# Float32 blocks first in each group of attention's value products

## The chip, the cores and the metric

The kernel runs on one core of one Trainium2 chip. The metric is device time in microseconds, the median of several runs. A profile of one execution stands beside them: for every instruction its engine, its start and its length. The engines are PE (matrix products, with its weight loads shown as PEld), DVE (vector work), ACT (activation functions, here mainly the exponential), POOL (general work) and SP (which starts DMAs).

## The reference

One input `x` of 2048 tokens by 640 features is normalised, goes through multi-head attention and through an MLP with a second normalisation, and all three are added up.

```
xn = _layernorm(x, axis=-1)
return x + _A_ref(xn, A_wqkv, A_wo) + _B_ref(xn, B_w1, B_b1, B_w2, B_b2)

# _A_ref: 32 heads of 20 features
scores = jnp.einsum("bhqd,bhkd->bhqk", q, k) * (Dh ** -0.5)
p = _softmax(scores, axis=-1)
o = jnp.einsum("bhqk,bhkd->bhqd", p, v)
```

`_B_ref` is a layer norm, a dense layer to 1536 features, GELU, and a dense layer back to 640.

## The kernel before

The kernel computes at about float32 accuracy. Most operands are split into an upper and a lower 16-bit half, and a product is the sum of several 16-bit products.

A first part normalises, transposes and projects to q, k and v. V goes to the tile `vfull`, by key blocks of 128 tokens: `SPLIT` (L25) marks two blocks of every four as split. A split block holds V as two float16 halves, the other two hold it as float32. With each head's 20 columns goes a column of ones, so that the products also give the softmax's sum.

Then comes attention, with the MLP and the output projection filled in between. Heads go in pairs: `(g, hf)` is a pair of heads and a half of the queries, `cc` one of two chunks of 512 queries in it, and `kb` a key block. A **unit** is one key block for one pair and one chunk. `scores` (L594) makes two products into a PSUM tile `s` (`psS` has three buffers) and ACT's exponential of it into a float32 tile `p` (L602), from the pool `ptp`, which has `2 * GRP - 1`, seven, buffers. For a split block, `rest` (L609) lets DVE subtract from `p` its upper bf16 half; the remainder is `low`, float16, with four buffers.

The **value products** of four units, a group (`GRP`), are made at once by `pv` (L619). All add up in one PSUM bank `o`, in four strips of 32 partitions: strip `q` has head `a = q // 2` of the pair, and `q % 2` keeps apart two partial sums. A product uses 32 columns of weights from `vfull`, so products on four strips can run side by side. For each split block and head there are two upper products (the upper half of `p`, read as bf16, with both halves of V) and one lower product (`low` with the upper half of V). A float32 block has one float32 product for each head. That makes 8 upper, 4 lower and 4 float32 products for a group, 256 groups in all. `start` is set on the first product of each strip in an accumulation over 16 blocks; after the last, ACT copies `o` to `ev` (L652).

The order around it is written out by hand. After scores of the second block of a group come the subtraction for the first block and a portion of filler (`other`); after scores of the fourth come the subtraction for the second block and then `pv(prev)`, the products of the group before. Filler is bounded by a credit, which grows by `rate` once a group. Filler is MLP work on PE (L823, L855) with its GELU on DVE and ACT (L758 to L770), and later the projection (L932).

So when the fourth exponential of a group is issued, the group's other three `p` tiles are in use and the four of the group before too. It takes the one that comes free first, by the order of the products in `pv(prev)`; the next three exponentials take the others in the order in which they come free. This is the loop:

```
for g, hf, cc, kb0 in groups:
    units = []
    for kb in range(kb0, kb0 + GRP):
        units.append([g, hf, cc, kb, scores(g, hf, cc, kb)])
...
        else:
            for u in units[1:]:
                rest(u)
            if prev:
                pv(prev)
...
    prev = units
```

Of the kernel before, what the change touches and what calls it, by code (L numbers as in the profile page):

```python
# [42 lines left out]
def mha_mlp_kernel(tc, x, wqkv, wo, w1, b1, w2, b2, out):  # L43
# [4 lines left out]
    with (  # L48
# [21 lines left out]
        vfull = keep.tile([P, PAD + NKB * VROW], F32, name="vfull")  # L70
# [441 lines left out]
        with ExitStack() as scope:  # L512
# [92 lines left out]
            def upper(pt):  # L605

                return pt.bitcast(BF16).rearrange("p a (n t) -> p a n t", t=2)[:, :, :, 1]
# [11 lines left out]
            def pv(units):  # L619

                g, hf, cc, kb0 = units[0][:4]
                if kb0 == 0:
                    pv.o = psO.tile([P, 512], F32, tag="o", name="o")
                    pv.begun = set()
                last = units[-1][3] == NKB - 1

                def product(q, src, v0, t):  # L630
                    nc.tensor.matmul(pv.o[32 * q : 32 * q + 32, :], src[:, v0 - PAD * (1 - q % 2) :][:, :32], t,  # L631
                                     start=q not in pv.begun, stop=last, skip_group_check=True)
                    pv.begun.add(q)

                split = [(u[3], upper(u[4]), u[5]) for u in units if SPLIT[u[3]]]
                whole = [(u[3], u[4]) for u in units if not SPLIT[u[3]]]
                of16 = lambda kb, a: 2 * PAD + kb * 2 * VROW + (2 * g + a) * 2 * VW
                of32 = lambda kb, a: PAD + kb * VROW + (2 * g + a) * VW
                for kb, up, _ in split:
                    for a in range(2):  # L640
                        product(2 * a, vhalf, of16(kb, a), up[:, a])
                        product(2 * a + 1, vhalf, of16(kb, a) + VW, up[:, a])
                for a in range(2):
                    for n, (kb, _, low) in enumerate(split):
                        product(2 * a + n % 2, vhalf, of16(kb, a), low[:, a])
                for a in range(2):
                    for n, (kb, pt) in enumerate(whole):
                        product(2 * a + n % 2, vfull, of32(kb, a), pt[:, a])
                if last:
                    if cc == 0:  # L650
                        evs[g, hf] = m1.tile([P, 2, 512], F32, tag="ev", name="ev")
                    nc.scalar.activation(evs[g, hf][:, cc], pv.o, AF.Copy)  # L652
                    if cc == 1:
                        unload(g, hf, evs.pop((g, hf)))
# [5 lines left out]
            def unload(g, hf, ev):  # L660
                cols = slice(hf * 1024, (hf + 1) * 1024)
                for p in range(2):
                    dma(g, hf)(lpart[p, hf, 2 * g : 2 * g + 2, :].rearrange("a (c t) -> a c t", c=2),
                                      ev[PAD + DH + VW * p :: 64])
                    for a in range(2):
                        q0, r = 64 * a + PAD + VW * p, (2 * g + a) * DH
                        dma(g, hf)(opart[p, r : r + DH, cols].rearrange("d (c t) -> d c t", c=2),
                                          ev[q0 : q0 + DH])
                if g + 1 in ENDS:
                    fins.append(finish(g + 1 - UNITS[ENDS.index(g + 1)], g + 1, hf))  # L670
                    if len(fins) == 1:

                        (sides if hf == 1 and g + 1 >= TAIL else patient).append(finishing())
# [289 lines left out]
            with tc.manual_schedule():  # L963
# [18 lines left out]
# [4 lines that stand above are left out]
                        if kb % 2 == 0:  # L986
                            continue
                        tick()
                        if kb % GRP == 1:

                            rest(units[0])
                            credit += rate
                            other()
# [7 lines that stand above are left out]
                                credit += rate  # L1003
                                other()
                    prev = units
                    if cc == 0 and kb0 == 0 and (g, hf) != ORDER[-1]:
                        n = ORDER[ORDER.index((g, hf)) + 1]
                        sides.append(load_stack(*n, *([stacks[g, hf][1]] if n[0] == g else [])))
                n = 0
# [12 lines left out]

                more(2)
                pv(prev)
                while more(1):
                    pass
# [102 lines left out]
```

## Time and profile before

| | us |
|---|---|
| median of three runs | 1376.91 (1376.67 to 1377.99) |
| the profiled execution, as timed | 1378.13 |
| its span in the profile | 1376.4 |
| PE busy | 1347.3 |
| ACT busy | 1125.5 |
| DVE busy | 1061.0 |

How to read the rows in what follows. A row of a group of instructions has the line of the kernel, the engine, the operation, the tile written and the tiles read, the shapes and the count; then the busy time in us and the mean length of one in ns; then the idle time of the engine just before, with what ended it. A row of waits has who waited for whom, the sum in us, the number of times and the longest. A row of the timeline has start and length in us, and equal neighbours merged with their count. A row of a window has its length and each engine's busy time in the order PE, PEld, DVE, ACT, POOL, then the granted clock of PE, the share of the DMA engines and GB/s. Ends of matrix products are modelled and neighbours overlap, so a short wait of PE can be hidden inside busy time.

### The profile page before, as it was taken

Reading aid. Unit: us, or ns where it says so; the run is one execution under the profiler, and the core shown is the slowest. Engines: PE = TensorE matmul, PEld = TensorE weight load, DVE = VectorE, ACT = ScalarE, POOL = GpSimd, SP = SyncE. Lnnn points to the kernel's source line nnn. Section 1 sums busy time; section 2 is a strip of 40 time slices with the busy share of each in tenths; the row PEclk is TensorE's granted clock in tenths of the full one; section 3 lists DMA queues with packets and bytes.
Section 4 is the critical chain, followed back from the end, with each engine's and each line's share of the span. In section 5 each row is a group of like instructions: output and inputs, shape, how many; then the busy total and the mean of one; then the engine's idle time right before and its main releaser. Section 6 shows DMA issues by size and latency. Waiting matters only on the chain.

```text
span 1376.4 us, 29091 instructions
## 1 busy us (share of the span) xinstructions
PE 1347.3 (98%) x11711; PEld 599.3 (44%) x11711; DVE 1061.0 (77%) x1425; ACT 1125.5 (82%) x1282; POOL 32.6 (2%) x75
## 2 busy tenths in 40 slices
PE   8999998999999999999999999999999999999998
PEld 6555555443334333433343333343434434333375
DVE  6647753899778988788888778887978898898732
ACT  5644332999999999999999999999999999999700
POOL 2000000000000000000000000000000000000000
PEclk9999999999999999999999999999999999999999
DMA  9853413012113222213231123232123222244275
GB/s 266 226 187 115 99 58 114 3 33 62 52 38 100 81 76 68 70 47 82 67 99 40 47 66 89 64 83 62 41 57 113 73 76 77 65 135 119 89 235 177
DMA packets 92320, 125.68 MB, mean 91 GB/s; under 512 B 16905, under 2 KB 58569, under 8 KB 92178
## 3 DMA queue, kind: packets, MB, share of 16 engines
q1 hardware_dynamic: 89218, 117.14, 28.9%
q0 software_dynamic: 2304, 5.24, 2.2%
q8 instruction: 94, 1.54, 0.5%
q10 hardware_dynamic: 656, 1.36, 0.3%
q14 instruction: 48, 0.39, 0.1%
HBM read 80.84 MB, written 42.86 MB: 90 GB/s over the span
## 4 chain that ended last, share of the span: by engine, by line
PE 66%; DVE 8%; ACT 3%; DMA 2%; issue 2%; SPq 1%; DVEq 0%; ACTq 0%
PE o L631 26%; PE s L600 16%; PE py L855 11%; PE pu L823 9%; PE z L932 4%; DVE low L614 3%; ACT p L602 3%; DVE u L758 1%; DVE u L759 1%; DVE w L762 1%; DMA oscr<-oa 1%; DMA acc<-accscr 0%; DVE w L763 0%; DVE hT L770 0%; DVE u L768 0%
## 5 line engine op out<-in xcount | busy, mean ns | idle before, releaser
L602 ACT ACTIVATE p<-s 128x1024 f32<-128x1024 f32 x1024 | 973.9, 1043 | 46.2 <-PE s L600 38.9
L614 DVE TENSOR_TENSOR low<-p 128x1024 f16<-128x1024 f32 x512 | 610.6, 1218 | 162.4 <-ACT p L602 161.7
L631 PE MATMUL o<-p,vfull 128*32 128x512 bf16 (+1 forms) x4096 | 430.2, 493 | 0.0
L600 PE MATMUL s<-qs,ks 61*128 61x512 f16 x2048 | 317.3, 382 | 7.0 <-ACT p L602 5.5
L600 PEld LDWEIGHTS <-ks 61*128 61x128 f16 x2048 | 64.0, 94 | 294.4 <-issue 291.9
L823 PE MATMUL pu<-xm,w1t 128*128 128x256 f16 x1440 | 181.1, 275 | 3.8 <-DMA xm<-xscr 2.7
L855 PE MATMUL py<-w2t,hT 128*128 128x320 f16 x1152 | 178.6, 300 | 1.7 <-DVE u L758 1.1
L823 PEld LDWEIGHTS <-w1t 128*128 128x128 f16 x1440 | 131.5, 98 | 72.1 <-issue 57.8
L855 PEld LDWEIGHTS <-hT 128*128 128x128 f16 x1152 | 102.5, 98 | 89.3 <-issue 55.1
L286 PE MATMUL qkp<-xnt,wv 128*128 128x512 f16 x600 | 132.5, 379 | 0.2 <-DVE wv L383 0.2
L631 PEld LDWEIGHTS <-vfull 128*32 128x32 f16 x3072 | 60.4, 95 | 137.7 <-issue 106.3
L631 PE MATMUL o<-low,vfull 128*32 128x512 f16 x1024 | 103.5, 378 | 3.7 <-DVE low L614 3.7
L300 ACT ACTIVATE qkhl<-qkp,qks 128x1024 f16<-128x1024 f32 (+1 forms) x24 | 23.3, 971 | 82.9 <-PE qkp L286 65.4
L286 PEld LDWEIGHTS <-wv 128*128 128x128 f16 x600 | 58.1, 98 | 68.2 <-DVE wv L383 0.7
L631 PEld LDWEIGHTS o<-p,vfull 128*32 128x32 f32 x2048 | 62.1, 108 | 52.3
L932 PE MATMUL z<-w1t,ot 128*128 128x320 f16 x480 | 66.3, 299 | 1.4 <-DMA ot<-oscr 0.8
L349 PE MATMUL vp<-wv,xnt 128*128 128x320 f16 x480 | 66.6, 299 | 0.0
L932 PEld LDWEIGHTS <-ot 128*128 128x128 f16 x480 | 46.5, 98 | 21.9 <-issue 2.9
L349 PEld LDWEIGHTS <-xnt 128*128 128x128 f16 x480 | 46.5, 98 | 18.2
L893 DVE SCALAR_TENSOR_TENSOR acc<-z,sc,acc 128x320 f32<-128x320 f32 x32 | 17.5, 550 | 46.8 <-PE z L932 42.7
L301 DVE SCALAR_TENSOR_TENSOR qkhl<-qkp,qks,qkhl 128x1024 f16<-128x1024 f32 (+1 forms) x24 | 26.5, 1104 | 32.2 <-ACT qkhl L300 32.2
L652 ACT ACTIVATE ev<-o 128x512 f32<-128x512 f32 x64 | 39.5, 618 | 3.5 <-PE o L631 3.5
(168 smaller groups left out, 682.6 us busy)
## 6 DMA issues: line engine op xcount, KB each, us to landing
qkscr<-qkhl SPq DMA_DIRECT2D x40, 256.0 KB
opart<-ev SPq DMA_DIRECT2D x124, 80.0 KB
ks<-qkscr SPq DMA_DIRECT2D x120, 80.0 KB
qs<-qkscr SPq DMA_DIRECT2D x192, 40.0 KB
oa<-opart SPq DMA_DIRECT2D x32, 240.0 KB
xt<-in_A_x_dram SPq DMA_DIRECT2D x16, 320.0 KB
xscr<-xnt SPq DMA_DIRECT2D x4, 1280.0 KB
xm<-xscr SPq DMA_DIRECT2D x8, 640.0 KB
```

The lines of the kernel that those rows point to most:

```text
L286: nc.tensor.matmul(ps[:, i, :], wv[:, k, q, a, mm * P : (mm + 1) * P], xnts[c][:, k, b, :], start=(k + n == 0), stop=(k == KD - 1 and n == 2))
L300: nc.scalar.activation(hl[:, 0, i0:i1], ps[:, i0:i1], AF.Copy, scale=a)
L301: nc.vector.scalar_tensor_tensor(hl[:, 1, i0:i1], ps[:, i0:i1], a, hl[:, 0, i0:i1], ALU.mult, ALU.subtract)
L349: nc.tensor.matmul(ps[:, hf, :320], xnts[c][:, k, a, j * P : (j + 1) * P], wv[:, k, 2, b, hf * 320 : (hf + 1) * 320], start=(n == 0), stop ...
L600: nc.tensor.matmul(ps[:, a, :], ks[64 * a : 64 * a + 61, kb * P : (kb + 1) * P], qs[64 * a : 64 * a + 61, cc * 512 : (cc + 1) * 512], star ...
L602: nc.scalar.activation(pt, ps, AF.Exp, scale=QS)
L614: nc.vector.tensor_sub(low, pt, upper(pt))
L631: nc.tensor.matmul(pv.o[32 * q : 32 * q + 32, :], src[:, v0 - PAD * (1 - q % 2) :][:, :32], t, start=q not in pv.begun, stop=last, skip_gr ...
L652: nc.scalar.activation(evs[g, hf][:, cc], pv.o, AF.Copy)
L823: nc.tensor.matmul(ps[:, i], w1v[:, k, (f + i) // 4, a, fo_ : fo_ + P], xnt[:, k, b, :], start=(n == 0), stop=(n == 3 * KD - 1))
L855: nc.tensor.matmul(ps[:, :320], hTs[mc][:, f, a, j * P : (j + 1) * P], w2v[:, f, b, hf * 320 : (hf + 1) * 320], start=(n == 0), stop=(n == ...
L932: nc.tensor.matmul(ps[:, :320], ot[:, k, a, j * P : (j + 1) * P], wov[:, k, b, h * 320 : (h + 1) * 320], start=(n == 0), stop=(n == 3 * KD ...
```

## The change

In `pv`, the loop over the float32 blocks is moved from the end to the beginning. The order in a group was upper, lower, float32; it becomes float32, upper, lower. The products are the same, with the same operands.

```diff
                 of32 = lambda kb, a: PAD + kb * VROW + (2 * g + a) * VW
+                for a in range(2):
+                    for n, (kb, pt) in enumerate(whole):
+                        product(2 * a + n % 2, vfull, of32(kb, a), pt[:, a])
                 for kb, up, _ in split:
                     for a in range(2):
                         product(2 * a, vhalf, of16(kb, a), up[:, a])
                         product(2 * a + 1, vhalf, of16(kb, a) + VW, up[:, a])
                 for a in range(2):
                     for n, (kb, _, low) in enumerate(split):
                         product(2 * a + n % 2, vhalf, of16(kb, a), low[:, a])
-                for a in range(2):
-                    for n, (kb, pt) in enumerate(whole):
-                        product(2 * a + n % 2, vfull, of32(kb, a), pt[:, a])
```

## The prediction

> **What bounds the kernel now.** I read the page first, then the groups of instructions kept apart by shape, then the waits, the chain of waits inside a quiet stretch, and last the timeline of single groups of value products.
>
> ```profile
> span 1376.4 us, 29091 instructions
> PE 1347.3 (98%) x11711; PEld 599.3 (44%) x11711; DVE 1061.0 (77%) x1425; ACT 1125.5 (82%) x1282; POOL 32.6 (2%) x75
> ...
> 240.00:1299.00 1059.00, 1046.07 (x9732) 418.45 (x9736) 895.25 (x1066) 1014.98 (x1141) 14.16 (x17) 1.00 0.25 70
> ...
> by line: PE o L631 40.0%; PE s L600 26.3%; PE py L855 18.6%; PE pu L823 14.2%; ACT p L602 1.0%; issue 0.1%
> ```
>
> The second-last row is the stretch of attention, from 240 to 1299 us: PE is busy for 1046 of 1059 us and ACT for 1015. The last row is the chain of waits between 600 and 700 us: 99% of it is PE, 1% is ACT. So PE sets the pace, ACT stands 3% behind it, and a change in the order of PE's work can count in two ways only: it lengthens or shortens PE's own time, or it makes PE wait for ACT or DVE.
>
> ```profile
> L602 ACT ACTIVATE p<-s 128x1024 f32<-128x1024 f32 x1024 | 973.9, 1043 | 46.2 <-PE s L600 38.9 <-ACT p L602 0.5
> L600 PE MATMUL s<-qs,ks 61*128 61x512 f16 x2048 | 317.3, 382 | 7.0 <-ACT p L602 5.5 <-ACT vfull L359 0.3
> L631 PE MATMUL o<-low,vfull 128*32 128x512 f16 x1024 | 103.5, 378 | 3.7 <-DVE low L614 3.7
> L652 ACT ACTIVATE ev<-o 128x512 f32<-128x512 f32 x64 | 39.5, 618 | 3.5 <-PE o L631 3.5
> L766 ACT ACTIVATE w<-w 128x512 f32<-128x512 f32 x48 | 30.6, 637 | 0.0
> ...
> ACT p L602 <- PE s L600: 38.9, 119, 2.4
> PE s L600 <- ACT p L602: 5.5, 18, 0.6
> PE o L631 <- DVE low L614: 3.7, 7, 0.8
> ```
>
> Both ways of waiting are there already. The exponentials wait for scores 119 times (38.9 us in all, 0.33 us each). Scores wait for exponentials 18 times (5.5 us), and value products wait for `low` 7 times (3.7 us). Since PE's ends are modelled, short waits hide in busy time; I come back to that.
>
> Here is one whole group in time; the 20 records of L631 are 8 upper products (bf16), 4 lower ones (f16) and 4 float32 ones of two passes each.
>
> ```profile
> 404.82 3.01 ACT L602 ACTIVATE p<-s 128x1024 f32<-128x1024 f32 x3
> 405.39 0.60 PE L600 MATMUL s<-qs,ks 61*128 61x512 f16 x4
> 405.93 0.64 PE L631 MATMUL o<-p,vfull 128*32 128x512 bf16 x8
> 406.40 0.39 PE L631 MATMUL o<-low,vfull 128*32 128x512 f16 x4
> 406.61 1.03 PE L631 MATMUL o<-p,vfull 128*32 128x512 f32 x8
> 407.57 0.61 PE L600 MATMUL s<-qs,ks 61*128 61x512 f16 x4
> 407.72 0.60 ACT L652 ACTIVATE ev<-o 128x512 f32<-128x512 f32 x1
> 408.21 2.86 ACT L602 ACTIVATE p<-s 128x1024 f32<-128x1024 f32 x3
> 408.88 0.80 PE L600 MATMUL s<-qs,ks 61*128 61x512 f16 x4
> 409.61 0.64 PE L631 MATMUL o<-p,vfull 128*32 128x512 bf16 x8
> ```
>
> The group takes 407.57 - 405.93 = 1.64 us of PE: 0.47 upper, 0.21 lower, 0.96 float32. Four products run side by side in the four column strips, so a wave of 16-bit products is 0.21 to 0.23 us. Four scores take 0.54 us up to the first upper product where two waves would be 0.44: 0.10 us is lost where the shape of the tiles changes. At the other end float32 has 0.96 us for two waves of 0.43: again 0.10.
>
> **The change part by part.** No instruction is added or removed, and no DMA is moved on a queue; the 256 groups issue the same 16 products each, with float32 at 0, upper at about 0.85 and lower at about 1.31 us.
>
> *PE's own time.* Before, a group has two changes of shape (scores to upper, float32 to scores); after, it has two (scores to float32, lower to scores). I cost them as equal, 0. The unknown is the first load after a change and the step from float32 to 16 bit within one shape.
>
> ```profile
> L631 PEld LDWEIGHTS o<-p,vfull 128*32 128x32 f32 x2048 | 62.1, 108 | 52.3
> L631 PEld LDWEIGHTS <-vfull 128*32 128x32 f16 x3072 | 60.4, 95 | 137.7 <-issue 106.3
> ...
> 111.99 0.63 PE L262 MATMUL pt<-ident,xt 128*128 128x128 f32 x4
> 112.35 0.48 PEld L349 LDWEIGHTS <-xnt 128*128 128x128 f16 x4
> 112.46 0.57 PE L349 MATMUL vp<-wv,xnt 128*128 128x320 f16 x3
> ```
>
> A float32 load is 108 ns, a 16-bit one 95: with the float32 load exposed first, 13 ns x 256 = +3.3 us at worst; the same with the other sign, -3.3, if the exposed end gets cheaper. In the last three rows float32 transposes are followed by 16-bit products of the same shape: the 16-bit load starts 0.11 us ahead of its product, under the last transpose, and four transposes take 0.47 us up to it, so nothing like 0.10 is lost. I take 0, the row being the nearest.
>
> *Lower products come later: a gain.* The lower products wait for DVE's subtraction of the second block, and where DVE is late the whole of PE stands.
>
> ```profile
> 319.11 0.64 PE L631 MATMUL o<-p,vfull 128*32 128x512 bf16 x8
> 319.21 3.49 DVE L614 TENSOR_TENSOR low<-p 128x1024 f16<-128x1024 f32 x3
> 319.57 0.38 PE L631 MATMUL o<-low,vfull 128*32 128x512 f16 x1
> 320.48 0.40 PE L631 MATMUL o<-low,vfull 128*32 128x512 f16 x3 [0.53 <-DVE low L614]
> 320.49 1.25 PE L631 MATMUL o<-p,vfull 128*32 128x512 f32 x8
> 320.89 0.62 ACT L766 ACTIVATE w<-w 128x512 f32<-128x512 f32 x1
> 321.67 0.60 PE L600 MATMUL s<-qs,ks 61*128 61x512 f16 x4
> 322.10 1.94 ACT L602 ACTIVATE p<-s 128x1024 f32<-128x1024 f32 x2 [0.58 <-PE s L600]
> ...
> 850.71 0.65 PE L631 MATMUL o<-low,vfull 128*32 128x512 f16 x4
> ...
> 1122.90 0.71 PE L631 MATMUL o<-low,vfull 128*32 128x512 f16 x4
> ...
> 1285.87 0.81 PE L631 MATMUL o<-low,vfull 128*32 128x512 f16 x4
> ```
>
> This group takes 321.67 - 319.11 = 2.56 us instead of 1.64: 0.92 lost, of which 0.53 shows as idle and 0.38 hides behind the first lower product. So the seven waits of the row cost 3.7 + 7 x 0.38 = 6.4 us. Three more stay wholly inside busy time: 0.65, 0.71 and 0.81 instead of 0.39 us, together 1.0. In all 7.4 us. With the lower products 1.31 - 0.47 = 0.84 us later, the longest (0.8 + 0.38 = 1.18) still waits 0.34, and those of 0.92 about 0.1: some 0.9 us stay for all ten. Gain 6.5 us. DVE's subtraction itself is not moved. I keep 6.0, because behind such a group the exponential, which waited 0.58 us for scores here, may find itself late in turn; the bounds are 6.5 and, if half is eaten, 3.
>
> *Buffers of p come free later: a loss.* There are seven buffers of `p` for groups of four. The fourth exponential of a group must take one that this very group of products (those of the group before) frees. Before, that is block 0, read by the first four upper products; in the changed program its wait stands on the third float32 product. In the timeline the three exponentials end at 407.83, so the fourth of its group starts 1.04 earlier, at 406.79: 0.86 us after the products' start, held by nothing but ACT. After, float32 ends 1.03 us after the start (the row of 1.03), and an exponential starts about 0.05 after what it waits for (scores' first pair at 321.67 + 0.38, exponential at 322.10): 1.08. Late by 1.08 - 0.86 = 0.2 us, in every group where ACT runs close behind PE; where ACT is late by itself, nothing. What is late next is the following exponential. Mostly it waits for scores anyway (119 waits, 0.33 us each) and swallows the 0.2. But where the `ev` copy (64 times) or the tanh (48 times) lies between, ACT has no idle time left, and the second pair of scores after that waits for a PSUM buffer: in the timeline above, scores at 408.88 take 0.80 instead of 0.60 us for this reason. There 0.2 goes straight onto PE.
>
> How often? 2048 score products are busy for 317.3 us; in 512 sets of 0.60 they would be 307.2. The 10.1 us between, at 0.2 us (what hides behind the first pair), are some 50 sets that wait for ACT now. About half, I estimate, follow a group where ACT was close behind: 25 x 0.2 = 5.0 us. Below: 0, if idle time swallows all. Above: all 112 copies and tanhs, 22 us. I take 5.0, nearest to the sets that wait today.
>
> *Free of charge:* the `ev` copy still waits for the group's last product, which ends at the same time since the group is as long; the lower products free their `low` buffers 0.84 us later, but four buffers for two per group leave a whole group of about 4 us as cover. The first product of an accumulation is now a float32 one and waits for the same `ev` copy as the upper one did.
>
> Sum: 0 - 6.0 + 5.0 = -1.0 us. The profiled execution took 1378.13 us (1376.4 span and 1.7 around it), so it would be 1377.1; it stands 1.2 above the median of 1376.91, and set against that median the forecast is **1375.9 us**.
>
> **The rivals.** *The late release is swallowed:* loss 0, gain 6.5, 1370.4 us. For it: 119 waits for scores stand behind exponentials. Against it: the 0.80 at 408.88.
>
> *ACT hands its delay to PE (slower):* at the scores behind an `ev` or a tanh, 0.2 us each. It decides from 30 of the 112 places on, where 6.0 us of gain are used up. At 56 it costs 11.2 - 6.0 = +5.2, 1382.1 us; at all 112, +16.4, 1393.3. For it: ACT is only 3% behind PE, and DVE and filler would find the same shift. Against it: only some 50 sets wait at all now.
>
> *16-bit weights are exposed behind float32 in the strips (slower too):* 95 ns x 256 = +24.3, less 1.0, 1400.2 us. Only the full-width transposes speak against it; the strips show no such step before. The Trainium skill (TensorE: Matmul & The Clock Gate, Step-by-step: what each phase is for) says that a load is pulled ahead of running matmuls when it goes to the background weight buffer; by that rule the load has a float32 pass of 0.43 us as cover, the transposes agree with their 0.11, and the sum stays as it is.
>
> *The change does not do what it says:* the pool could hand out buffers so that nothing moves, or the ten waits could lie off the chain; 1376.9 us. The built program, where the fourth exponential waits on another product, speaks against it.
>
> **How the numbers follow.** The sum as it stands: 0.48, its own range 1371 to 1381 (gain 3 to 6.5, loss 0 to 8, PE's own time within 3.3). Swallowed: 0.17. ACT hands on: 0.25. Weights exposed: 0.05. Nothing: 0.05. A measurement tells about 0.2%, 2.7 us, from no change. Faster than 1374.2: 0.17 from the swallowed case, 0.16 of the first. Same: 0.24 of the first, 0.05 of nothing. Slower than 1379.7: 0.08 of the first, 0.25, 0.05. The range goes from the first case's lower end and the swallowed one's 1370.4, less a little for PE's own time, to between 56 and 112 paying places: 1369 to 1388.
>
> **What would show it.** The row of value products waiting for `low` should fall from 3.7 us to under 1. The exponentials' rows should show waits for L631, which they do not have now, and start about 1.08 us after the first float32 product. The waits of scores for ACT should grow from 5.5 us, and the float32 products should stay at 592 ns with the first upper one 0.85 behind. A group longer than 1.64 us between waits would mean exposed weights. The forecast is wrong if DVE's lateness moves along with the products, or if PE waits for ACT in far more than 50 sets.

## The result and the profile after

| | before | after |
|---|---|---|
| median, us | 1377.99 (1376.42 to 1382.32, 7 runs) | 1384.88 (1383.55 to 1388.93, 7 runs) |
| profiled execution, as timed | 1378.13 | 1384.04 |
| its span | 1376.4 | 1382.3 |

The ratio is 1.0051, with a 95% interval of 1.0034 to 1.0067: slower by 0.5%, some 7 us. The forecast was 1 us faster.

First the groups of instructions of the changed kernel, kept apart by shape, then the rows of its waits:

```profile
L602 ACT ACTIVATE p<-s 128x1024 f32<-128x1024 f32 x1024 | 981.3, 1042 | 46.0 <-PE o L631 25.8 <-PE s L600 17.9
L600 PE MATMUL s<-qs,ks 61*128 61x512 f16 x2048 | 321.4, 382 | 12.2 <-ACT p L602 10.9 <-ACT vfull L359 0.3
L631 PE MATMUL o<-p,vfull 128*32 128x512 f32 x2048 | 273.1, 605 | 0.0
L631 PE MATMUL o<-low,vfull 128*32 128x512 f16 x1024 | 102.4, 377 | 0.0
```

```profile
ACT p L602 <- PE o L631: 25.8, 99, 0.6
ACT p L602 <- PE s L600: 17.9, 43, 2.2
PE s L600 <- ACT p L602: 10.9, 35, 0.7
```

Three things stand out. The lower products show no wait any more (3.7 us before). Exponentials now wait 99 times for value products, a releaser that they did not have; their idle time as a whole is 46.0 us as it was, so ACT's own row shows no damage. But scores wait for ACT for 10.9 us instead of 5.5, and float32 passes have a mean of 605 ns instead of 592. This was their row in the kernel before:

```profile
L631 PE MATMUL o<-p,vfull 128*32 128x512 f32 x2048 | 266.6, 592 | 0.0
```

The chain of waits between 600 and 700 us, by line, shows the same from the other side: ACT's exponential had 1.0% of it and has 7.5%.

```profile
by line: PE o L631 38.5%; PE s L600 23.6%; PE py L855 15.3%; PE pu L823 13.1%; ACT p L602 7.5%; issue 1.5%; ACT ev L652 0.7%; ACT w L766 0.2%; ACTq L602 0.1%
```

Now the timeline of the same group of products as in the prediction, with the `ev` copy behind it (float32 and upper products stand merged in one row of 16):

```profile
404.42 0.61 PE L600 MATMUL s<-qs,ks 61*128 61x512 f16 x4
...
404.95 1.52 PE L631 MATMUL o<-p,vfull 128*32 128x512 f32 x16
...
406.13 1.02 ACT L602 ACTIVATE p<-s 128x1024 f32<-128x1024 f32 x1 [0.25 <-PE o L631]
406.29 0.40 PE L631 MATMUL o<-low,vfull 128*32 128x512 f16 x4
...
406.62 0.61 PE L600 MATMUL s<-qs,ks 61*128 61x512 f16 x4
407.05 0.59 ACT L652 ACTIVATE ev<-o 128x512 f32<-128x512 f32 x1
...
407.52 4.70 ACT L602 ACTIVATE p<-s 128x1024 f32<-128x1024 f32 x5
...
407.92 0.39 PE L600 MATMUL s<-qs,ks 61*128 61x512 f16 x2
...
408.61 0.39 PE L600 MATMUL s<-qs,ks 61*128 61x512 f16 x2 [0.30 <-ACT p L602]
```

The fourth exponential starts at 406.13, 1.18 us after the products' start, where it started at 0.86 to 0.88 before. The `ev` copy and the next exponential follow it without a gap, and the second pair of scores starts 0.69 us after the first where 0.22 is usual: 0.47 lost, against 0.19 at this place before. The group itself is 406.62 - 404.95 = 1.67 us long, not 1.64.

And the group in which DVE's subtraction was late (2.56 us before):

```profile
317.59 1.52 PE L631 MATMUL o<-p,vfull 128*32 128x512 f32 x16
317.70 3.49 DVE L614 TENSOR_TENSOR low<-p 128x1024 f16<-128x1024 f32 x3
...
318.77 1.02 ACT L602 ACTIVATE p<-s 128x1024 f32<-128x1024 f32 x1 [0.25 <-PE o L631]
318.93 0.44 PE L631 MATMUL o<-low,vfull 128*32 128x512 f16 x4
...
319.30 0.61 PE L600 MATMUL s<-qs,ks 61*128 61x512 f16 x4
```

DVE is as late as it was, three operations in a row for 3.49 us, but the group takes 319.30 - 317.59 = 1.71 us: 0.85 us are gained.

To add this up I measured three quantities in the trace of each kernel, from start to start of PE's records, so that modelled ends play no part. *Length*: from the last scores before a group's products to the first scores after them, median over 254 groups. *Late lower*: the sum of what groups take over that median, differences under 0.02 us left out. *Late scores*: the sum of what the second pair of scores in the latter half of a group takes over its usual 0.223 us, with the number of places, differences under 0.01 us left out. The last column is the row of exponentials that wait for value products.

| kernel | time against before, us | length, us | late lower, us | late scores, us | exponentials waiting, us |
|---|---|---|---|---|---|
| before | | 1.951 | 7.6 | 11.7 (44) | 0 |
| after | +7.0 | 1.972 | 0.7 | 20.7 (70) | 25.8 (99) |

256 x 0.021 = +5.4, 0.7 - 7.6 = -6.9, 20.7 - 11.7 = +9.0. The sum is +7.5 us, and +7.0 was measured (0.0051 x 1378).

### The profile page after: what moved, and what is told of

It is laid out like the page before. It is cut to its first block, busy times and chain, and to the rows that moved or that the text cites. A ratio compares the mean times of both kernels' runs of the same rounds, so it can differ in the third digit from the quotient of the medians.

```text
span 1382.3 us, 29110 instructions
## 1 busy us (share of the span) xinstructions
PE 1352.6 (98%) x11711; PEld 611.8 (44%) x11711; DVE 1061.8 (77%) x1425; ACT 1132.8 (82%) x1282; POOL 32.3 (2%) x75
## 4 chain that ended last, share of the span: by engine, by line
PE 76%; DVE 10%; ACT 9%; issue 2%; DMA 2%; SPq 0%; ACTq 0%; POOL 0%; DVEq 0%
PE o L631 24%; PE s L600 15%; PE pu L823 9%; PE py L855 9%; PE qkp L286 8%; ACT p L602 8%; PE vp L349 4%; DVE low L614 4%; PE z L932 4%; PE pt L262 1%; DVE u L758 1%; DMA ks<-qkscr 1%; ACT ev L652 0%; DMA acc<-accscr 0%; DVE u L759 0%
## 5 line engine op out<-in xcount | busy, mean ns | idle before, releaser
L602 ACT ACTIVATE p<-s 128x1024 f32<-128x1024 f32 x1024 | 981.3, 1042 | 46.0 <-PE o L631 25.8
L631 PE MATMUL o<-p,vfull 128*32 128x512 f32 (+1 forms) x4096 | 388.6, 496 | 0.0
L600 PE MATMUL s<-qs,ks 61*128 61x512 f16 x2048 | 321.4, 382 | 12.2 <-ACT p L602 10.9
L631 PEld LDWEIGHTS <-vfull 128*32 128x32 f16 x3072 | 90.5, 97 | 185.2 <-issue 157.1
L600 PEld LDWEIGHTS <-ks 61*128 61x128 f16 x2048 | 66.8, 94 | 202.2 <-issue 201.4
L631 PE MATMUL o<-low,vfull 128*32 128x512 f16 x1024 | 102.4, 377 | 0.0
L631 PEld LDWEIGHTS o<-p,vfull 128*32 128x32 f32 x2048 | 40.6, 108 | 92.4 <-issue 92.4
```

The lines of the kernel that those rows point to most:

```text
L600: nc.tensor.matmul(ps[:, a, :], ks[64 * a : 64 * a + 61, kb * P : (kb + 1) * P], qs[64 * a : 64 * a + 61, cc * 512 : (cc + 1) * 512], star ...
L602: nc.scalar.activation(pt, ps, AF.Exp, scale=QS)
```

## The experiments

The theory is this accounting: an exposed float32 load (a weight load that starts only with its product, not under the product before it), a wait of PE for DVE that is saved, and a buffer of `p` that is late. The first rival is that the waits of exponentials have only changed their name, since ACT's idle sum is the same, so that the exposed load is all that slows the kernel. The second is that the lateness of lower products is not saved but moves elsewhere. Eight kernels were run, each beside the kernel before on the same chip.

### e1: upper, float32, lower

```diff
                         product(2 * a + 1, vhalf, of16(kb, a) + VW, up[:, a])
+                for a in range(2):
+                    for n, (kb, pt) in enumerate(whole):
+                        product(2 * a + n % 2, vfull, of32(kb, a), pt[:, a])
                 for a in range(2):
                     for n, (kb, _, low) in enumerate(split):
                         product(2 * a + n % 2, vhalf, of16(kb, a), low[:, a])
-                for a in range(2):
-                    for n, (kb, pt) in enumerate(whole):
-                        product(2 * a + n % 2, vfull, of32(kb, a), pt[:, a])
```

> Order upper, float32, lower. The accounting (three terms: +5.6 us because the float32 weight load is exposed behind scores, 22 ns in each of 256 groups; about -6.8 us because lower products no longer wait for DVE; +9 us because the fourth exponential's buffer of p comes free late and PE then waits for ACT) expects the first and third term gone and the second kept: about 7 us faster than the kernel before, group length back at 1.64 us, no exponential waiting for L631, scores waiting for ACT no more than the 5.5 us of before. The rival, that the new waits of exponentials for products only carry another name (ACT's idle time before exponentials is 46 us in both kernels) and that the lateness of lower products comes back elsewhere, expects no change against the kernel before, within 2 us.

Measured: 1371.66 us, ratio 0.9953 (0.9939 to 0.9968), 6.5 us faster than before. The groups of instructions of this kernel:

```profile
L602 ACT ACTIVATE p<-s 128x1024 f32<-128x1024 f32 x1024 | 974.1, 1047 | 41.3 <-PE s L600 34.3 <-ACT p L602 0.5
...
L600 PE MATMUL s<-qs,ks 61*128 61x512 f16 x2048 | 317.5, 382 | 7.2 <-ACT p L602 5.7 <-ACT vfull L359 0.3
L631 PE MATMUL o<-p,vfull 128*32 128x512 f32 x2048 | 264.1, 591 | 0.0
...
L631 PE MATMUL o<-low,vfull 128*32 128x512 f16 x1024 | 100.7, 378 | 0.0
```

No exponential waits for products, scores wait 5.7 us, float32 is back at 591 ns, and the lower products do not wait. So the saved wait is a real gain, and both losses go away when 16-bit products of block 0 come first. This order beats both kernels.

### e2: a late buffer without the exposed load

Four upper products come first, of block 0 for one head and of block 1 for the other. So neither block's buffer is free before float32.

```diff
+                for a in range(2):
+                    kb, up, _ = split[a]
+                    product(2 * a, vhalf, of16(kb, a), up[:, a])
+                    product(2 * a + 1, vhalf, of16(kb, a) + VW, up[:, a])
                 for a in range(2):
                     for n, (kb, pt) in enumerate(whole):
                         product(2 * a + n % 2, vfull, of32(kb, a), pt[:, a])
-                for kb, up, _ in split:
-                    for a in range(2):
-                        product(2 * a, vhalf, of16(kb, a), up[:, a])
-                        product(2 * a + 1, vhalf, of16(kb, a) + VW, up[:, a])
+                for a in range(2):
+                    kb, up, _ = split[1 - a]
+                    product(2 * a, vhalf, of16(kb, a), up[:, a])
+                    product(2 * a + 1, vhalf, of16(kb, a) + VW, up[:, a])
```

(This one is shown against the changed kernel.)

> First four upper products (block 0 for the first head, block 1 for the second), then float32, then the other four upper products, then lower. No float32 load stands behind scores, so the group should be 1.64 us again; but no buffer of p is free before the float32 products' third, now one wave (0.2 us) later than in the changed kernel. The accounting: -6.8 us from the lower products, and the fourth exponential late by about 0.5 instead of 0.3 us, so PE's waits for ACT cost 15 us or more instead of 9: some 8 to 14 us slower than the kernel before. The rival, that late release costs nothing and the cold load is what made the changed kernel slower: 5 to 7 us faster than the kernel before.

Measured: 1397.98 us, ratio 1.0136 (1.0120 to 1.0152), 18.7 us slower. The groups of this kernel, and two rows of its timeline:

```profile
L602 ACT ACTIVATE p<-s 128x1024 f32<-128x1024 f32 x1024 | 974.9, 1031 | 63.3 <-PE o L631 44.0 <-PE s L600 13.7 <-ACT p L602 0.2
...
L600 PE MATMUL s<-qs,ks 61*128 61x512 f16 x2048 | 325.7, 382 | 23.1 <-ACT p L602 21.1 <-ACT vfull L359 0.3
```

```profile
406.55 1.50 PE L631 MATMUL o<-p,vfull 128*32 128x512 bf16 x16
...
407.94 1.94 ACT L602 ACTIVATE p<-s 128x1024 f32<-128x1024 f32 x2 [0.36 <-PE o L631]
```

The fourth exponential starts 407.94 - 406.55 = 1.39 us after the products, 0.51 later than before; scores wait for ACT 21.1 us. The first rival falls: the load is not exposed here (float32 passes have a mean of 591 ns), and the late buffer alone costs more than in the changed kernel. The size was above the expected 8 to 14: 0.21 us more delay cost another 14.7 us (late scores 35.4 instead of 20.7), at 110 places instead of 70. That ACT has no idle time left at the new places is how I read it; it was not tried by itself.

### e3 and e4: eight buffers of p, in the order of before and in the changed one

```diff
-        ones = keep.tile([P, P], F32, name="ones")
+        ones1 = keep.tile([P, 1], F32, name="ones")
+        ones = ones1.to_broadcast([P, P])
...
-            ptp = pool(name="pt", bufs=2 * GRP - 1)
+            ptp = pool(name="pt", bufs=8)
...
-                        rb = m1.tile([P, 512], F32, tag="rb", name="rb")
+                        rb = o0
...
-                    for h in range(0 if last else nh):
+                    for h in range(0):
...
-                    nc.vector.tensor_mul(o0, o0, rb)
+                    (nc.vector.tensor_mul if last else nc.vector.tensor_sub)(o0, o0, rb if last else o0)
```

> The order of before, with eight buffers of p in place of seven. Room is made by leaving out the broadcast of the softmax's reciprocal sums and the product with it (a subtraction of the same size is done in its place, so attention's share is missing from the output except for the last heads), and by reading the tile of ones as a broadcast column. No wait of an exponential for value products existed before, so the accounting expects the eighth buffer to change little: within 3 us of the kernel before. It is the reference for the next run.

> The same with the changed order (float32, upper, lower). With eight buffers no exponential waits for the products of the group before. The accounting: +5.6 for the exposed load, -6.8 for the lower products, 0 for the release: 0 to 3 us faster than the run with eight buffers in the order of before. The rival, that late release costs nothing: still 6 to 7 us slower than that run.

To make room, both kernels, and e5 below, leave out the product with the softmax's reciprocal sums, so their output lacks attention's share except for the last heads.

Measured: 1377.95 us, ratio 0.9999 (0.9987 to 1.0011), and 1377.06 us, ratio 0.9998 (0.9985 to 1.0012). With eight buffers the two orders cannot be told apart. The groups of the changed order with eight buffers (its lines are one further down):

```profile
L603 ACT ACTIVATE p<-s 128x1024 f32<-128x1024 f32 x1024 | 972.6, 1041 | 45.0 <-PE s L601 42.3
...
L601 PE MATMUL s<-qs,ks 61*128 61x512 f16 x2048 | 317.7, 382 | 7.1 <-ACT p L603 6.5 <-ACT vfull L360 0.3
L632 PE MATMUL o<-p,vfull 128*32 128x512 f32 x2048 | 273.0, 605 | 0.0
```

The waits for products are gone, and the waits of scores for ACT are back at 6.5 us. The float32 passes are still at 605 ns, so that part does not depend on the buffers. This is the plainest evidence for the late buffer: one more buffer takes the 7 us away, and e3 shows that neither it nor what is left out changes the time in the order of before.

### e5: eight buffers, upper, float32, lower

The edit of e1 on top of e3.

> Eight buffers of p (with the same part left out: the softmax's reciprocal sums and the product with them, a subtraction in its place), order upper, float32, lower. Against the eight-buffer run in the order of before only the place of the lower products differs: the accounting expects 6 to 7 us less. Against the eight-buffer run in the changed order only the exposed float32 load differs: the accounting expects 5 to 6 us less, so the price of that load alone. If the exposed load is free, it is within 2 us of that run.

Measured: 1373.89 us, ratio 0.9962 (0.9947 to 0.9976), 5.2 us below the kernel before. Against e3 that is 5.1 us for the place of the lower products (6 to 7 expected), and against e4 5.0 us for the exposed load (5 to 6 expected). Each ratio is uncertain by up to 2 us on either side and a difference of two by some 2.5, so 5.1 cannot be told from 6 to 7. The length of a group is 1.951 us here and 1.972 in e4, and 256 x 0.021 = 5.4.

### e6: lower, upper, float32

```diff
+                for a in range(2):
+                    for n, (kb, _, low) in enumerate(split):
+                        product(2 * a + n % 2, vhalf, of16(kb, a), low[:, a])
                 for kb, up, _ in split:
```

The loop over the lower products is taken away further down.

> Order lower, upper, float32. If the late subtraction of DVE is what stalls PE, and its time does not move with the products, the waits seen in the trace of before would grow from about 7 to about 19 us with the lower products due at the start instead of 0.47 us later: some 10 to 14 us slower than the kernel before, the exponentials not waiting for products. If the lateness moves along with the products, no change, within 2 us.

Measured: 1388.75 us, ratio 1.0076 (1.0053 to 1.0100), 10.5 us slower. The waits of this kernel:

```profile
ACT p L602 <- PE o L631: 7.8, 11, 1.3
PE o L631 <- DVE low L614: 7.0, 10, 1.2
PE s L600 <- ACT p L602: 5.2, 17, 0.6
```

Value products wait 7.0 us visibly, and 18.4 us by the measure of start to start. DVE's lateness stays where it is, and what it costs depends on when the products ask. The second rival falls. One detail missed: 11 exponentials do wait for products, those behind a group that DVE held up.

### e7: float32 between the two upper blocks

```diff
-                for kb, up, _ in split:
+                for kb, up, _ in split[:1]:
                     for a in range(2):
                         product(2 * a, vhalf, of16(kb, a), up[:, a])
                         product(2 * a + 1, vhalf, of16(kb, a) + VW, up[:, a])
```

The same loop over `split[1:]` follows float32, and lower is last.

> Order upper of block 0, float32, upper of block 1, lower. The first buffer of p comes free as early as before; the others come free some 0.6 us or more later. If only the fourth exponential of a group is pressed for its buffer, this is as fast as the order upper, float32, lower: 5 to 7 us faster than before. If every buffer's release counts, it is slower than that order by 3 us or more.

Measured: 1373.46 us, ratio 0.9954 (0.9937 to 0.9971), 6.3 us faster, as fast as e1. No exponential waits for products in its trace. Only the first buffer to come free is pressed; the next exponentials start late enough for theirs.

### e8: float32, lower, upper

The two 16-bit parts of the changed kernel change places.

> Order float32, lower, upper. Exposed load +5.4 us and late release +9 us as in the changed kernel; the lower products are due at about 0.89 us instead of 1.34, where the trace of before has about 3.3 us of lateness beyond instead of 0.6: the accounting expects 9 to 11 us slower than before, 2 to 4 us slower than the changed kernel. If the lower products' place does not matter, it equals the changed kernel.

Measured: 1389.02 us, ratio 1.0070 (1.0051 to 1.0089), 9.7 us slower. Exponentials wait for products as in the changed kernel (26.4 us), and the late lower products cost 3.6 us instead of 0.7.

### All together

| kernel | time against before, us | length, us | late lower, us | late scores, us | sum of the three terms, us |
|---|---|---|---|---|---|
| after | +7.0 | 1.972 | 0.7 | 20.7 (70) | +7.5 |
| e1 upper, float32, lower | -6.5 | 1.951 | 0.8 | 12.1 (46) | -6.4 |
| e2 crossed | +18.7 | 1.959 | 0.8 | 35.4 (110) | +18.9 |
| e3 eight, before | -0.1 | 1.950 | 7.8 | 11.4 (45) | -0.4 |
| e4 eight, after | -0.3 | 1.972 | 0.6 | 12.2 (46) | -1.1 |
| e5 eight, upper, float32, lower | -5.2 | 1.951 | 0.8 | 11.8 (46) | -6.7 |
| e6 lower first | +10.5 | 1.958 | 18.4 | 11.0 (39) | +11.9 |
| e7 float32 between | -6.3 | 1.952 | 0.8 | 12.7 (47) | -5.5 |
| e8 float32, lower, upper | +9.7 | 1.972 | 3.6 | 20.2 (69) | +9.9 |

The times are (ratio - 1) x the median of before. The last column is each kernel's three terms minus those of before, worked out as above; it comes within 1.5 us of every time. The terms are read from each kernel's own trace, so this table accounts for the times and does not forecast them.

## Why the prediction was wrong

The three terms were the right ones, and the place of each was right. Two of the three sizes were wrong, both to the same side, and the sum of terms near each other's size changed its sign: -1.0 was forecast, +7.0 came. The time lies within the stated range of 1369 to 1388, but above the 1371 to 1381 of the sum itself. By the prediction's own chances, slower than 1379.7 had 0.38, more than faster (0.33) or the same (0.29), so its single number was not its likeliest case.

*PE's own time: forecast 0, within 3.3 either way; measured +5.4. This step failed.* The prediction weighed both unknowns, the step from float32 to 16 bit and the load that is exposed behind scores. The first was read rightly from the transposes: from the second float32 pass to the first upper product it takes 0.43 us, no more than a float32 pass itself. For the second, it had the difference of two load lengths, 108 - 95 = 13 ns a group or +3.3 us, and then took 0, because nothing was lost in the row of the transposes. But that row was of the other step and had nothing to say on this one.

These are the loads behind scores in the changed kernel, and then in e1:

```profile
404.95 0.16 PEld L631 LDWEIGHTS o<-p,vfull 128*32 128x32 f32 x8 [0.42 <-issue]
...
402.98 0.12 PEld L631 LDWEIGHTS <-vfull 128*32 128x32 f16 x8 [0.42 <-issue]
402.98 1.50 PE L631 MATMUL o<-p,vfull 128*32 128x512 bf16 x16
403.23 0.34 PEld L631 LDWEIGHTS o<-p,vfull 128*32 128x32 f32 x8
```

In both kernels the first load starts with its product (404.95 and 402.98), so in both it is exposed. The float32 loads of e1, at 403.23, start 0.23 us ahead of theirs. In the changed kernel the first float32 passes are at 617 ns and the second ones at 592, and from the first to the second it takes 0.454 us instead of 0.428: 26 ns lost. But 16-bit products in this place lose something too: their first wave takes 0.239 us, before and in e1, where the next one takes 0.226: 13 ns lost. So float32 behind scores costs some 13 ns more than 16 bit there, as much as the two loads differ by, and these 3.3 us should have stood in the sum. Another 6 ns were in no term: from the lower products to scores it takes 0.329 us in the changed kernel and 0.323 in e1. There the four strips start over 20 ns instead of 11, as they do from the first float32 pass on; whether that is the reason was not tried. The remaining 2 of the 21 ns lie in the steps between. (617 and 592 ns are means of the records; the times from one step to the next are medians over 254 groups, from start to start.)

*The lower products: forecast -6.0; measured -6.9.* The reading of hidden waits (0.38 us behind the first lower product, three groups without any visible idle time) gave 7.4 us; start to start it is 7.6. The deduction of 0.5 for an exponential that may find itself late was not needed.

*The late buffer: forecast +5.0; measured +9.0. This step was mis-sized.* The delay was 0.30 us (1.18 against 0.88) and not 0.2. Of the missing 0.1, some 0.03 is the slower first pass and the spread of the four starts, which put the third product's end at 1.06 us instead of 1.03, and 0.07 is that 0.12 instead of 0.05 us go by from that end to the exponential. The count was near for the places that pay in full: against the same set of scores in the kernel before, 22 lose more than 0.2 us, 0.28 on average and 6.2 in all, and 21 of them stand behind an `ev` copy, one of the two places that the prediction had named (it took 25 at 0.2). What it left out is small losses elsewhere: 41 more sets lose 0.02 to 0.2 us, 3.0 in all, and 25 of these stand behind neither a copy nor a tanh.

Of the rivals, the slower one, in which ACT hands its delay to PE, is what happened in kind, but it does not explain the 7 us by itself: 9.0 less the 6.9 gained is +2.1, and the rest is PE's own time. Its 0.25 should have been more, since the gain and the loss were within each other's error, and the two unknowns of PE's own time were not even: by the rows of 108 and 95 ns, one of them could only cost. The swallowed release (0.17) was wrong; e2 shows that the delay is not swallowed. Weights exposed behind float32 in the strips (0.05) did not happen: the 16-bit loads start at 405.41 and the first upper product at 405.84. The sign that was to show them, a group longer than 1.64 us, came all the same (1.67), from the float32 load behind scores.

What was to be seen came about in part: the wait for `low` under 1 us, exponentials waiting for L631, scores waiting for ACT more than 5.5 us. Not as forecast were the float32 mean of 592 ns and the start at 1.08 us.

## What to carry to other kernels

When a pool has one buffer less than the tiles in flight, the order of the readers decides which buffer comes free first, and with it how close the writer may run: here the block whose products are done soonest has to come first. Put products that wait for a late engine last, and those that free a buffer first; the order upper, float32, lower does both and is 6.5 us faster than the kernel before. And where idle time of the second engine is the same before and after, look at who ended it: of 46 us, 39 had been ended by scores, and after the change 26 were ended by value products.

## What the runs showed of the hardware

A wait costs more when it stands in an instruction of its own. Where the wait for scores is carried by the exponential, it starts 42 ns after the modelled end of scores (median of 97 cases, the first exponential of a group, before). Where the wait for scores stands in a separate wait instruction ahead, because the exponential itself carries another one, it starts after 102 ns (median of 100 cases, the third of a group, before). In e4 it is the third exponential that carries its wait itself, and it starts after 41 ns, while the first has the separate instruction and starts after 102; so it goes with the instruction and not with the place in the group. The fourth exponential of the changed kernel has its wait for float32 in such a separate instruction and starts 117 ns after the product's modelled end; how much of that is the wait instruction was not tried by itself.

Between scores (61*128) and value products (128*32), PE loses about 0.1 us in either direction. From the last pair of scores to the products it takes 0.31 us where one pair follows another after 0.23; from float32 to scores it takes 0.54 us before, where a pass is 0.43. The first products after scores lose a little more: 13 ns in a 16-bit wave and 26 in a float32 pass, with loads of 95 and 108 ns. Why the steps after it take 8 ns more in the changed kernel stays open.
